# Residual on VectorE and the SyncE queue for one more kind of the last outputs of a fused attention and mixer block

## The chip, the cores and the metric

One Trainium2 chip, one core. TensorE multiplies matrices, VectorE and ScalarE work element by element, and SyncE and POOL (GpSimd) here mostly issue DMAs, which are copies between the memories; a DMA "lands" when its completion is signalled. The metric is the device time of one execution in microseconds (us), the median of several runs. A profile is one execution taken by the hardware profiler; its span (first to last instruction) is some 1.8 us shorter than the reported time.

## The reference, cut to what matters

```python
h  = x + A(layernorm(x))          # linear attention with an output projection, S=2048, D=1024
h2 = h + B(layernorm(h))          # token mixer: gelu(h^T @ w1 + b1) @ w2 + b2, F=3584
```

What matters is the last addition: every element of the output is the mixer's second product plus a bias b2, plus the residual `h`. The output is bf16, 2048 x 1024.

## The kernel before

`h` is written to the output tensor in DRAM half way through the kernel. The second product then works on "quads": two pairs of 128-row blocks, by a Strassen-like scheme with seven products. A pair `p` gives four outputs of 128 x 512, named by (`sh`, `dh`): row block and column half. Most of them are added to the residual by the DMA itself (an accumulating write, which the kernel issues from POOL). In the last quad, the two outputs of kind (1, 0), which come last of all, are treated otherwise: the residual is fetched back from DRAM ahead of time, VectorE adds it, and SyncE issues a plain write.

```python
def fetch(self, sh, dh):                       # read the residual into dead rows of an old weight tile
    t = odd[self.p - 2][:, 0:2, :].rearrange("p a b -> p (a b)")
    i = 2 * self.p + sh
    hd.dma_start(t, o_dram[i * P:(i + 1) * P, dh * CW:(dh + 1) * CW])      # SyncE
    self.hr[sh, dh] = t

def out(self, sh, dh, a, b, op):
    i = 2 * self.p + sh
    if (sh, dh) in self.hr:
        r = 2 + 2 * (a > 0)
        ot = odd[self.p - 2][:, r:r + 2, :].rearrange("p a b -> p (a b)")
    else:
        ot = ots.pop(0)
        ots.append(ot)
    op(ot[:, a:b], b2_sb[:, i:i + 1])          # evacuation with bias: ScalarE, or VectorE for kind (1, 1)
    to = o_dram[i * P:(i + 1) * P, dh * CW + a:dh * CW + b]
    if (sh, dh) in self.hr:
        dve.tensor_tensor(ot[:, a:b], ot[:, a:b], self.hr[sh, dh][:, a:b], ALU.add)
        nc.sync.dma_start(to, ot[:, a:b])
    else:
        nc.gpsimd.dma_start(to, ot[:, a:b], accum_op=ALU.add)              # POOL
# ... in run2, for the last quad only (cut is not None):
                sts[-1].split(cut)             # the very last output in 384 and 128 columns
                for st in sts:
                    st.fetch(1, 0)
```

`dve` and `hd` keep VectorE and SyncE instructions in program order. The kinds come in the order (1, 1), (0, 0), (0, 1), (1, 0); the (0, 1) evacuations of the two pairs stand on both sides of the last addition of a small product (`psI`) on VectorE.

## Time and profile before

| | kernel before |
|---|---|
| time, median of 3 runs | 560.86 us (560.84 to 561.08) |
| span of the profile | 559.3 us |
| TensorE busy | 553.0 us (99%) |
| end of the last matmul to end of span | 4.49 us |
| POOL DMA issues of outputs | 30 |

TensorE never waits between 40 us and its last matmul, so the time is the start-up, a solid block of matmuls, and a **tail**: from the end of the last matmul group in the timeline (551.65 + 3.20 = 554.85) to the end of the span (559.35). The lines themselves stand in the prediction. (The prediction counts 4.9 us, from 554.48. That is where the chain leaves TensorE for the 384-column part of the last output; the matmuls of the 128-column part run on to 554.86, and the 0.59 us of ScalarE read there belong to the 384 columns.)

### The profile page before, as it was taken

Reading aid. Unit: us, or ns where it says so; the run is one execution under the profiler, and the core shown is the slowest. Engines: PE = TensorE matmul, PEld = TensorE weight load, DVE = VectorE, ACT = ScalarE, POOL = GpSimd, SP = SyncE. Lnnn points to the kernel's source line nnn. Section 1 sums busy time; section 2 is a strip of 40 time slices with the busy share of each in tenths; the row PEclk is TensorE's granted clock in tenths of the full one; section 3 lists DMA queues with packets and bytes.
Section 4 is the critical chain, followed back from the end, with each engine's and each line's share of the span. In section 5 each row is a group of like instructions: output and inputs, shape, how many; then the busy total and the mean of one; then the engine's idle time right before and its main releaser. Section 6 shows DMA issues by size and latency. Waiting matters only on the chain.

```text
span 559.3 us, 8827 instructions
## 1 busy us (share of the span) xinstructions
PE 553.0 (99%) x3339; PEld 316.2 (57%) x3339; DVE 435.3 (78%) x848; ACT 291.1 (52%) x617; POOL 28.0 (5%) x38
## 2 busy tenths in 40 slices
PE   8999999999999999999999999999999999999996
PEld 3444444454444444456766766666444667667664
DVE  6898888544777688889989789887997879749745
ACT  5747677766767877646456465464210413413222
POOL 1000000000000000000000000000002103103112
PEclk9999999999999999999999999999999999999999
DMA  9933342115774762102240440413869649849334
GB/s 306 297 76 76 80 90 39 19 36 203 223 203 136 241 202 76 75 1 85 69 150 5 147 134 18 151 46 88 206 203 237 197 137 245 206 131 229 86 95 66
DMA packets 83627, 74.25 MB, mean 133 GB/s; under 512 B 15602, under 2 KB 76032, under 8 KB 83584
## 3 DMA queue, kind: packets, MB, share of 16 engines
q1 hardware_dynamic: 78528, 69.09, 41.1%
q0 software_dynamic: 4384, 3.95, 5.3%
q10 hardware_dynamic: 672, 0.66, 0.3%
q8 instruction: 26, 0.43, 0.3%
q14 instruction: 17, 0.14, 0.1%
HBM read 58.86 MB, written 11.67 MB: 126 GB/s over the span
## 4 chain that ended last, share of the span: by engine, by line
PE 97%; DVE 2%; ACT 1%; issue 0%; DVEq 0%
PE psI L230 25%; PE acc_t L230 18%; PE psC L230 16%; PE psB L230 8%; PE psB L945 4%; PE psC L945 4%; PE psA L945 4%; PE acc_t L869 2%; PE acc_t L1231 2%; PE psB L342 2%; PE psA L342 2%; PE psE L945 2%; PE psC L342 2%; PE psA L230 1%; PE kvps L898 1%; PE psE L342 1%
## 5 line engine op out<-in xcount | busy, mean ns | idle before, releaser
L230 PEld LDWEIGHTS <-is 128*128 128x128 f16 x736 | 71.8, 98 | 31.2 <-DVE hi L230 0.4
L230 PEld LDWEIGHTS <-sa 128*128 128x128 f16 x606 | 59.2, 98 | 27.1
L230 PEld LDWEIGHTS <-wq 128*128 128x128 bf16 (+1 forms) x496 | 48.5, 98 | 28.1 <-issue 1.0
L230 PE MATMUL acc_t<-wo_sb,pqT 128*128 128x512 f16 x256 | 55.6, 379 | 0.0
L488 POOL DMA_DIRECT2D out_dram<-wq x30 | 26.1, 927 | 525.4 <-ACT wq L491 495.0
L230 PE MATMUL acc_t<-xnT,wq_sb 128*128 128x512 bf16 x192 | 43.4, 379 | 0.0
L230 PEld LDWEIGHTS <-pqT 128*128 128x128 bf16 x256 | 25.0, 98 | 30.5 <-issue 0.6
L193 DVE TENSOR_SCALAR e_sb<-e_sb 128x512 bf16<-128x512 bf16 x64 | 18.6, 290 | 28.7 <-ACT e_sb L189 28.1
L230 DVE TENSOR_TENSOR t<-psI,t 128x256 f32<-128x256 f32 (+1 forms) x45 | 20.8, 475 | 22.2 <-PE psI L230 20.9
L189 ACT ACTIVATE e_sb<-acc_t 128x512 bf16<-128x512 f32 x40 | 23.9, 597 | 24.5 <-PE acc_t L230 12.0
L230 PE MATMUL psC<-gs,wq 128*128 128x512 f16 x140 | 34.1, 379 | 0.0
L945 PEld LDWEIGHTS <-xs 128*128 128x128 f16 x208 | 20.0, 98 | 23.4 <-DVE xs L931 1.3
L230 PEld LDWEIGHTS <-wq_sb 128*128 128x128 bf16 x192 | 18.5, 98 | 23.0 <-issue 1.3
L230 PE MATMUL psC<-hT,sa 128*128 128x512 f16 x112 | 31.2, 379 | 0.0
L230 PE MATMUL psI<-hi,is 128*128 128x256 f16 x200 | 30.0, 273 | 0.0
L230 PE MATMUL psB<-hT,sa 128*128 128x512 f16 x112 | 29.7, 379 | 0.0
L230 DVE BATCH_NORM_STATS2 hst<-acc_t 128x6 f32<-128x512 f32 x32 | 21.4, 692 | 9.0 <-ACT h_bf L230 8.9
L945 PE MATMUL psA<-wkv,xnT 128*128 128x512 bf16 x104 | 26.7, 379 | 0.0
L945 PEld LDWEIGHTS <-xnT 128*128 128x128 bf16 x156 | 15.2, 98 | 18.5 <-issue 0.2
L230 PE MATMUL psC<-hT,wq 128*128 128x512 f16 x96 | 24.6, 379 | 0.0
L230 ACT CAST h_bf<-acc_t 128x512 bf16<-128x512 f32 x32 | 18.4, 582 | 11.9 <-PE acc_t L230 11.5
L230 ACT COPY psI<-psI 128x256 f32<-128x256 f32 x50 | 18.0, 360 | 11.6 <-PE psI L230 9.7
(229 smaller groups left out, 1090.2 us busy)
## 6 DMA issues: line engine op xcount, KB each, us to landing
wq<-in_B_w_dram SPq DMA_DIRECT2D x14, 1024.0 KB, 8.0
wq<-in_B_w_dram SPq DMA_DIRECT2D x12, 896.0 KB, 7.1
gs<-parked SPq DMA_DIRECT2D x9, 896.0 KB, 4.6
xr<-in_A_x_dram SPq DMA_DIRECT2D x16, 256.0 KB, 5.9
rdb<-rd_dram SPq DMA_DIRECT2D x32, 128.0 KB, 3.8
out_dram<-h_bf SPq DMA_DIRECT2D x16, 256.0 KB, 2.0
x_sb<-in_A_x_dram SPq DMA_DIRECT2D x15, 256.0 KB, 3.0
out_dram<-wq POOLq DMA_DIRECT2D x30, 128.0 KB, 4.7
```

The costliest lines, as they stand in the source:

```text
L189: pin(nc.scalar.activation(e_sb[:], src, ACT.Exp))
L193: pin(nc.vector.tensor_scalar(e_sb[:], e_sb[:], 1.0, PHI_EPS, ALU.min, ALU.add))
L230: return (lambda *a, **kw: pin(op(*a, **kw))) if self.always or getattr(Held, self.key) else op
L342: pe.matmul(ps[:, cols], lhsT=lhs[:, k, :], rhs=mv(k)[:, cols], start=(start and k == 0), stop=(k == self.nk - 1), skip_group_check=True,)
L488: nc.gpsimd.dma_start(to, ot[:, a:b], accum_op=ALU.add)
L869: mm = nc.tensor.matmul(pp[:, 0:CW], lhsT=xnT[:, kt, i * P:(i + 1) * P], rhs=wkv[:, kt, c * CW:(c + 1) * CW], start=(kt == 0), stop=(kt == ...
L898: pin(nc.tensor.matmul(kv_ps[b][:, sl, :], lhsT=pks[i % NPK][:, j * P:(j + 1) * P], rhs=vaugs[i % NVA][:, j, :], start=False, stop=(i == N ...
L945: pin(nc.tensor.matmul(ps[:], lhsT=lhs[:, k, :], rhs=rhs[:, k, :], start=(start and k == 0), stop=(k == hk2 - 1), skip_group_check=True,))
L1231: nc.tensor.matmul(qp[:, 0:SW], lhsT=wq_sb[:, kt, j * P:(j + 1) * P], rhs=xnT[:, kt, u * SW:(u + 1) * SW], start=(kt == 0), stop=(kt == ND ...
```

## The change

Its intent: take the last accumulating writes out of the tail, by giving the kind (0, 1), last but one, the treatment that (1, 0) has. The whole diff:

```diff
-            t = odd[self.p - 2][:, 0:2, :].rearrange("p a b -> p (a b)")
+            t = odd[self.p - 2][:, 6 * dh:6 * dh + 2, :].rearrange("p a b -> p (a b)")
...
-                r = 2 + 2 * (a > 0)
+                r = 6 * dh + 2 + 2 * (a > 0)
...
                 for st in sts:
+                    st.fetch(0, 1)
                     st.fetch(1, 0)
```

Two accumulating POOL writes go; two SyncE reads, two VectorE additions and two SyncE writes come.

## The prediction

> **What bounds the kernel now.** I read the page first (busy shares, then the chain that ended last), then that chain again for the last 9 us alone, then the timeline of the same stretch engine by engine, then the DMA view for its last 3.3 us, and last the instructions of the program's closing line (L1739), which carries the end barrier.
>
> ```profile
> PE 553.0 (99%) x3339; PEld 316.2 (57%) x3339; DVE 435.3 (78%) x848; ACT 291.1 (52%) x617; POOL 28.0 (5%) x38
> ...
> PE 97%; DVE 2%; ACT 1%; issue 0%; DVEq 0%
> ```
>
> The first line is busy time per engine, the second the chain's shares. TensorE is busy for 553 of 559.3 us and makes up 97% of the chain; the clock row of the page is full in every slice. The change touches no matmul. So only two places can pay: a stall of TensorE, or the tail after its last matmul. The chain of the last 9 us, in order of time, shows where the tail begins:
>
> ```profile
> 551.82 2.66 PE psC L230 x14
> 554.48 0.02 issue
> 554.50 0.59 ACT wq L491
> 555.09 0.02 issue
> 555.12 0.36 DVE wq L230
> 555.48 0.14 DVEq L1739
> ```
>
> The matmuls end at 554.48; ScalarE adds the bias to the last output (0.59), VectorE adds the residual (0.36), and this view then stops, because transfers are not instructions. The span ends at 559.3, so 3.7 us of the tail are writes and barrier. The timeline (start, length, engine, line) gives the writes:
>
> ```profile
> 551.60 1.49 ACT L491 ACTIVATE wq<-e,b_sb 128x512 bf16<-128x512 f32 x2 [5.33 <-DVE e L230]
> 551.65 3.20 PE L230 MATMUL psC<-gs,w2o 128*128 128x512 f16 x21
> 551.85 0.42 DVE L230 TENSOR_TENSOR e<-psI,e 128x256 f32<-128x256 f32 x1 [0.29 <-PE psI L230]
> 552.61 1.75 POOL L488 DMA_DIRECT2D out_dram<-wq  x2 [5.29 <-ACT wq L491]
> 553.37 0.69 ACT L491 ACTIVATE wq<-psC,b_sb 128x512 bf16<-128x512 f32 x1 [0.28 <-PE psC L230]
> 554.09 0.43 DVE L230 TENSOR_TENSOR wq<-wq 128x512 bf16<-128x512 bf16 x1 [1.81 <-ACT wq L491]
> 554.50 0.84 ACT L491 ACTIVATE wq<-psC,b_sb 128x384 bf16<-128x384 f32 x2 [0.45 <-PE psC L230]
> 554.54 1.81 SPq L486 DMA_DIRECT2D out_dram<-wq  x3
> ```
>
> The two POOL issues at 552.61 are the accumulating writes that the change removes. In the trace they land at 555.70 and 557.21, and their packets are on the DMA engines until 556.84. The three SyncE writes (128, 96, 32 KB), issued at 554.54, 555.50 and 555.94, land at 557.39, 557.72 and 557.88. So the last landing is the 32 KB write's, but both kinds share the engines, as the DMA view of the last stretch shows (q0 is POOL's queue, q1 SyncE's):
>
> ```profile
> q1 hardware_dynamic: 420, 0.25, 25.2%
> q0 software_dynamic: 71, 0.06, 10.9%
> issues: line engine op xcount, KB each, median us to landing
> out_dram<-wq SPq DMA_DIRECT2D x1, 32.0 KB, 1.9
> ```
>
> After 557.88 comes the end barrier. In the instructions of L1739 (duration min/median/max in ns, first and last start in us):
>
> ```profile
> L1739 SPq EVENT_SEMAPHORE  x9: 17/28/28, 557.2 to 558.3; - x9
> ...
> L1739 POOLq DRAIN  x1: 5204/5204/5204, 553.4 to 553.4; - x1
> ```
>
> SyncE checks nine pairs of DMA semaphores one after another, some 0.06 us apiece, and is through at 558.40; POOL's drain, begun at 553.36, lasts 5.20 us and ends at 558.56, later than SyncE. The barrier steps after it take the span to 559.35.
>
> **What the Trainium skill says.** "DMA: Bandwidth & Descriptors", section Anatomy of one DMA, puts the fixed cost of a DMA at about 2 us, most of it the write receipt. The trace is a little below: 1.70 to 1.73 us for the 128 KB writes of the reciprocals to DRAM by SyncE, 2.0 us for the 256 KB residual writes in a quiet stretch. The same page, section Queues, rings and completion order, says that each DMA engine serves its queues in turn, packet by packet. The trace agrees in effect: the 128 KB write at 554.54 took 2.85 us beside POOL's packets. "Perfetto Trace Analysis", section DMA Instruction — SWDGE (GPSIMD), says that the profiled time of a POOL DMA is descriptor generation, not movement: here 0.86 us shown, 3.1 and 3.8 us to landing. "VectorE: DVE Perf Modes", section on the SBUF errata, measures a fixed term near 150 cycles; with two bf16 elements a cycle, 512 columns are an estimate of (150 + 256)/0.96 = 423 ns, and the trace has 0.43 us.
>
> **The change part by part.** The instruction order of the changed build, compared with the old one, is the same on TensorE; only the end of the others differs.
>
> *Fetches.* Two more 128 KB reads of the residual beside two of the same size, issued by SyncE near 537.8 at 0.47 us each. They queue behind the 896 KB reload of gs (issued 537.38, landed 542.18; first wanted by TensorE at 544.03), so they delay it little, and they are wanted only at 552.3. By the landings of the present two (542.52, 542.85) the new ones land near 543.5. Cost on the path: 0. The new tiles lie in weight rows that are already dead.
>
> *VectorE.* Two additions of 0.43 us, in program order. The first comes before the last psI sum, which now waits for ScalarE: add 552.35 to 552.78 (ScalarE ends the first output at 552.32), sum to about 553.12 (was 552.28), second activation 553.15 to 553.88 (was 552.36 to 553.08). The psC activation waits for ScalarE, 553.8 to 554.5 instead of 553.37 to 554.05: 0.45 us later. The 384-column one still starts at 554.50, as its matmuls end at 554.48. The sum's bank is wanted by no later matmul. So the delay is used up just ahead of the last output: 0 to 0.1 us on the path.
>
> *SyncE issues.* Five writes instead of three: about 552.8, 554.4, 555.0, 555.50, 555.94. An issue takes 0.34 to 0.41 us, so the last two stay where they are.
>
> *POOL.* Two issues of 0.87 us go, and its drain starts some 6 us earlier.
>
> *Landing of the last write.* Without POOL's packets, a quiet SyncE write shows its first packet 0.83 us after issue and lands 0.35 us after its last packet (a residual write at 217.64: packets 218.47 to 219.30, landed 219.65). The 32 KB write has 8 packets on each engine at 18 ns, 0.15 us; with some spread, 0.83 + 0.25 + 0.38 = 1.46 us instead of 1.94: landing at 557.40 instead of 557.88, **-0.48**.
>
> *End barrier.* SyncE's DMAs take the eight hardware semaphores in turn. The last write has the second of them now; four more issues move it to the sixth. In the present trace six more checks follow its own; then there will be two: 4 x 0.06 = **-0.25**. And POOL's drain, if it depends only on POOL's own DMAs, no longer ends after SyncE: 558.56 against an arrival of about 558.43, **-0.13**.
>
> Sum: -0.48 - 0.25 - 0.13 + 0.05 = -0.81 us at the most optimistic. I don't give the drain and the landing their full value and take -0.65: 560.86 - 0.65 = 560.2.
>
> **The rivals.** (1) The landing is hidden anyway: the 32 KB write is a receipt-bound write that POOL's traffic hardly touches (1.94 us against 1.70 for a bigger one in quiet). Then only the barrier pays, 0.1 to 0.4 us: 560.5 to 560.8. (2) The serial chain between VectorE and ScalarE becomes the end: if the activations follow each other with more delay than I counted, the last two SyncE issues slip by 0.1 to 0.4 us and eat the gain: 560.5 to 561.0. For it: four handovers between the two engines now stand in a row before 554.5. Against it: about 0.45 us of idle ScalarE time before 554.50 covers them. (3) The extra reads delay the gs reload and TensorE stalls near 544: up to 0.6 us for 256 KB at the 430 GB/s seen then, so about 561.4; against it, 1.85 us of slack and the order of issue.
>
> **Range and chances.** The whole tail after the last matmul is 4.9 us of 560.86; 2% is 11.2 us. No part of the change can give that, and none adds it. Runs of the kernel before differ by 0.24 us, so I take 559.8 to 560.7: the low end is the full sum and a bit of luck between runs, the high end rival 1 or 2 with little left. Faster by over 2%: 0.01; within 2%: 0.985; slower: 0.005.
>
> **What would show it.** Right: matmuls still end near 554.5; POOL's last issue is near 546; five SyncE writes, the last issued within 0.1 us of 555.94, with a landing near 1.5 us; span near 558.6. Wrong: a TensorE gap between 542 and 546 (rival 3), a last SyncE issue after 556.1 (rival 2), a 32 KB landing still at 1.8 us or more (rival 1), or a POOL drain that ends just after SyncE's checks again, which would mean that it never was a cost of its own.

## The result, and the profile after

| | before | after |
|---|---|---|
| median of 3 runs | 560.86 us (560.84 to 561.08) | 560.33 us (560.04 to 561.04) |
| ratio, 95% interval | | 0.9992 (0.9969 to 1.0014) |
| the same, timed again (9 and 6 runs) | 561.02 us (560.31 to 561.79) | 560.22 us (560.01 to 562.66) |
| ratio, 95% interval | | 0.9984 (0.9970 to 0.9997) |
| span of the first profile | 559.3 us | 558.3 us |
| tail of the first profile | 4.49 us | 3.65 us |

A ratio is the mean time of one kernel's runs over that of the other's of the same rounds, so not quite the ratio of the medians. As point estimates the gain is 0.5 to 0.9 us, within 2%. The first interval includes no gain at all; the second goes from 0.2 to 1.7 us.

The timeline of the kernel after, in the stretch and with the columns of that shown before (start, length, engine, line, operation, count, idle time before it):

```profile
551.36 0.72 ACT L491 ACTIVATE wq<-e,b_sb 128x512 bf16<-128x512 f32 x1 [5.33 <-DVE e L230]
551.42 3.20 PE L230 MATMUL psC<-gs,w2o 128*128 128x512 f16 x21
552.12 0.42 DVE L230 TENSOR_TENSOR wq<-wq 128x512 bf16<-128x512 bf16 x1 [0.79 <-ACT wq L491]
552.46 0.42 DVE L230 TENSOR_TENSOR e<-psI,e 128x256 f32<-128x256 f32 x1
552.57 3.52 SPq L486 DMA_DIRECT2D out_dram<-wq  x5
552.91 0.72 ACT L491 ACTIVATE wq<-e,b_sb 128x512 bf16<-128x512 f32 x1 [0.83 <-DVE e L230]
553.54 1.57 ACT L491 ACTIVATE wq<-psC,b_sb 128x512 bf16<-128x512 f32 x3
553.67 1.00 DVE L230 TENSOR_TENSOR wq<-wq 128x512 bf16<-128x512 bf16 x2 [0.79 <-ACT wq L491]
554.88 0.49 DVE L230 TENSOR_TENSOR wq<-wq 128x384 bf16<-128x384 bf16 x2 [0.22 <-ACT wq L491]
```

There is no POOL line any more, and five SyncE writes instead of three. VectorE, ScalarE and VectorE wait for one another in turn (0.79, 0.83, 0.79 us), as the order of instructions had it. Yet the 384-column activation starts 0.35 us ahead of the last matmul's end in both kernels, and the last VectorE pair 0.26 us after it in both: the handovers were absorbed.

The DMA view from 555.8 us to the end, and the instructions of the program's closing line (duration min/median/max in ns, then first and last start in us):

```profile
q1 hardware_dynamic: 353, 0.18, 25.3%
issues: line engine op xcount, KB each, median us to landing
out_dram<-wq SPq DMA_DIRECT2D x1, 32.0 KB, 1.6
```

```profile
L1740 SPq EVENT_SEMAPHORE  x10: 17/28/28, 556.1 to 557.6; - x10
L1740 POOLq DRAIN  x3: 51/102/5622, 545.8 to 558.0; - x3
```

POOL's queue q0 is gone from the last stretch; the 32 KB write lands 1.6 us after its issue instead of 1.9. POOL's long drain begins at 545.8 and is over 5.6 us later, long before the end.

All 14 profiles can be put into one table. Times are in us from the end of the last matmul: issue of the last write, how long it takes to land, when SyncE is through its checks of the DMA semaphores (the counters that a landing raises; two short drains of SyncE are counted in), when POOL's drain ends (one instruction of the program's closing line, on which POOL stays until after its own last DMA has landed), and the tail. Where POOL's drain was over before the last matmul, there is a dash.

| kernel | issue | landing takes | SyncE through | drain ends | tail |
|---|---|---|---|---|---|
| before | 1.08 | 1.94 | 3.55 | 3.70 | 4.49 |
| before, again | 1.08 | 1.70 | 3.31 | 3.52 | 4.31 |
| after | 1.03 | 1.57 | 2.88 | - | 3.65 |
| after, again | 1.03 | 1.56 | 2.87 | - | 3.64 |
| before, checks turned by four | 1.04 | 1.75 | 3.07 | 3.32 | 4.11 |
| after, plain writes by POOL | 1.08 | 1.73 | 3.22 | 3.29 | 4.08 |
| after, one tiny late POOL write | 1.03 | 1.57 | 2.88 | 2.96 | 3.75 |
| second pair only | 1.07 | 1.57 | 3.04 | 2.20 | 3.81 |
| after, turned by two | 1.03 | 1.57 | 2.76 | - | 3.53 |
| after, turned by three | 1.03 | 1.57 | 3.18 | - | 3.95 |
| after, one more VectorE addition | 1.41 | 1.57 | 3.26 | - | 4.04 |
| after, last write from ScalarE | 0.79 | 1.75 | 2.82 | - | 3.59 |
| after, one operation per output | 0.73 | 1.56 | 2.55 | - | 3.32 |
| all three together | 0.61 | 1.63 | 2.40 | - | 3.17 |

One rule, read off these profiles, fits every row to 0.01 us: the tail is 0.745 us (the barrier, from POOL's step that waits for everybody to the end of the span) after the later of two arrivals, SyncE through its checks plus 0.025, or POOL's drain plus 0.045. In the kernel before, and in the three experiments whose last POOL DMA is issued within 1.5 us of the last matmul's end, it is POOL's; else SyncE's.

### The profile page after: what moved, and what is told of

Same layout as the page of the kernel before. It is cut to its first block, busy times and chain, and to the rows that moved or that the text cites. A ratio compares the mean times of both kernels' runs of the same rounds, so it can differ in the third digit from the quotient of the medians.

```text
span 558.3 us, 8814 instructions
## 1 busy us (share of the span) xinstructions
PE 551.9 (99%) x3323; PEld 315.8 (57%) x3339; DVE 436.1 (78%) x850; ACT 291.0 (52%) x617; POOL 26.3 (5%) x36
## 4 chain that ended last, share of the span: by engine, by line
PE 95%; DMA 2%; DVE 2%; issue 1%; ACT 0%; DVEq 0%
PE psI L230 25%; PE acc_t L230 18%; PE psC L230 16%; PE psB L230 8%; PE psC L946 4%; PE psB L946 4%; PE psA L946 4%; PE psB L342 2%; PE psA L342 2%; PE acc_t L1232 2%; PE psE L946 2%; DMA x_sb<-in_A_x_dram 2%; PE psC L342 2%; PE acc_t L870 2%; PE psA L230 1%; PE kvps L899 1%
## 5 line engine op out<-in xcount | busy, mean ns | idle before, releaser
L488 POOL DMA_DIRECT2D out_dram<-wq x28 | 24.4, 928 | 519.8 <-ACT wq L491 489.5
```

## The experiments

My theory: the tail has two paths in parallel. POOL: last POOL write, landing, drain. SyncE: last write, landing, checks. The change takes POOL out, and makes SyncE's path shorter by quiet engines and by fewer checks after the last landing. Rivals: the 0.5 us are noise of the start; it is the accumulating kind of DMA that costs, whatever the queue; the drain only follows SyncE.

### Both kernels again

No edit. The kernel after was timed in five rounds; the kernel before was profiled once more.

> The changed kernel again, timed in five rounds. The tail is counted from the end of the last matmul group in the timeline to the end of the span: 4.50 us in the kernel before (554.85 to 559.35), 3.65 in the one profile of the changed kernel (554.62 to 558.27). My theory (the 0.85 us are a fixed saving in the tail): tail 3.6 to 3.7 again, ratio of times 0.9980 to 0.9990, whole interval below 1. Rival (the 0.5 us between the medians are run to run noise of the front, as runs of 560.04, 561.04 and 560.33 suggest): tail between 3.7 and 4.5, ratio 0.9995 to 1.0005.

> The kernel before once more, for a second tail. If tails are fixed by the program: 4.45 to 4.55 us, last write issued 1.1 us after the last matmul's end, landing 1.9 us later, POOL's drain ending after SyncE's checks. If they vary from run to run as the whole times do: off by 0.2 us or more.

The tail of the kernel after came out as 3.64, 0.01 from the first, and the ratio as 0.9984 with an interval below 1: theory. The tail of the kernel before was 4.31, not 4.45 to 4.55. That is the first miss, and a useful one: issue and checks were the same to 0.01 us, but POOL's last write landed 2.17 us after the last matmul instead of 2.36, and SyncE's last one took 1.70 instead of 1.94. So in these two pairs the landings vary in the kernel with POOL's writes (1.94, 1.70) and hardly in the one without (1.57, 1.56).

In the longest run, which happened to be profiled, the start is to blame. The run of the kernel after that was profiled here took 562.66 us; its waits of TensorE name the place:

```profile
PE acc_t L870 <- DMA wkv<-in_A_wqkv_dram: 2.2, 1, 2.2
PE acc_t L98 <- DVE warm L88: 1.2, 1, 1.2
PE psB L946 <- DVE xs L932: 0.3, 1, 0.3
```

The first line, 2.2 us of waiting for the first weights, is absent in all other profiles but one, the plain writes by POOL below, where it is 0.3 us. Comparing the start of the same ScalarE instruction in this profile and the first one of the kernel after, the shift is 2.6 us at 30 us and still 2.6 us at the end. Between the first profiles of before and after it is 0.23 us, at 30 us and at the end alike. So of the 1.08 us between those two spans, 0.23 come from the start, which the change doesn't touch, and 0.85 are the change.

### Turning the order of the checks in the kernel before

SyncE's DMAs take eight hardware semaphores in turn, and at the end the semaphores are checked in a fixed order. Four dead reads (8 KB each; nobody uses what they bring) shift which one the last write has.

```diff
                 for st in sts:
                     st.fetch(1, 0)
+                for k in range(4):
+                    hd.dma_start(odd[sts[0].p - 2][:, 12, 32 * k:32 * (k + 1)], x[0:P, 32 * k:32 * (k + 1)])
```

> The kernel before with four tiny dead reads by SyncE ahead of its last writes, so that the last write has the sixth semaphore in turn as in the changed kernel, and two checks follow its own instead of six. SyncE should be through its checks about 0.28 us after the last landing, not 0.53. Theory (POOL's drain depends only on POOL's own DMAs, some 1.3 us after the last of them lands, and gates the end): tail unchanged, 4.45 to 4.55. Rival (the drain only follows SyncE, so the checks set the end): tail 4.2 to 4.3.

SyncE was through 0.28 us after its last landing instead of 0.53, at 3.07. The end did not follow it: POOL's drain ended 0.25 us later, at 3.32, and the tail was that plus 0.79. From the closing line:

```profile
L1741 SPq DRAIN  x3: 7/7/13, 557.9 to 558.5; - x3
L1741 POOLq DRAIN  x2: 102/2460/4819, 553.4 to 558.4; - x2
L1741 POOLq EVENT_SEMAPHORE  x2: 17/17/17, 558.2 to 558.3; - x2
```

SyncE's first drains stand at 557.9; POOL's long one runs from 553.37 for 4.82 us to 558.19, and the barrier step that waits for everybody (POOL EVENT_SEMAPHORE) comes right after it, at 558.2. So the drain doesn't follow SyncE, and by the order of arrivals a shorter row of checks alone gains nothing in the kernel before, as long as POOL's drain is later. The tail itself doesn't show that: it was 4.11, below the 4.45 to 4.55 of the theory and even below the 4.2 to 4.3 of the rival, since POOL's last write landed at 1.97 this time. Whether the dead reads had a part in this, one profile can't say. In all three profiles of this family the drain ends 1.35 us after that landing.

### Plain writes by POOL

```diff
-                nc.sync.dma_start(to, ot[:, a:b])
+                (nc.gpsimd if dh else nc.sync).dma_start(to, ot[:, a:b])
```

> The changed kernel, whose two (0,1) outputs take the residual on VectorE as there, but leave by POOL as plain writes (result right). Theory (the gain comes from POOL being out of the tail: its packets beside the last write and its late drain): POOL's last issue is near 1 us before the last matmul's end, lands some 2 to 3 us later, drain 1.3 us after that; landing of the last write 1.6 to 1.9 us; tail 4.2 to 4.7. Rival (the gain comes from the accumulating kind of DMA being gone, whatever the queue): tail 3.6 to 3.9.

The tail was 4.08, between the two ranges: 0.12 below the theory's, 0.18 above the rival's. POOL's two issues, from the timeline (the last matmul ends at 555.26 here):

```profile
553.48 0.57 POOL L486 DMA_DIRECT2D out_dram<-wq  x1 [5.74 <-DVE wq L230]
555.03 0.56 POOL L486 DMA_DIRECT2D out_dram<-wq  x1 [0.98 <-DVE wq L230]
```

The second one is issued 1.24 us later against the last matmul than in the kernel before, as it waits for VectorE's addition, but it lands after 2.18 us instead of 3.83, so POOL is done 0.2 to 0.4 us earlier (landing at 1.94 against 2.36 and 2.17). The accumulating kind does cost landing time here, but without it half of the gain or more is still missing: the tail is 0.43 us longer than that of the kernel after. Not all of this is the drain. This version has SyncE's last write on the fourth semaphore (four checks after its own), which accounts for 0.12; its landing is 0.17 longer and its issue 0.05 later; by the rule above only the last 0.10 are the drain's, which arrives that much after SyncE.

### One tiny late POOL write

```diff
                 nc.sync.dma_start(to, ot[:, a:b])
+                if dh and self.p % 2:
+                    nc.gpsimd.dma_start(dram.tile([P, 32], BF16, name="scratch")[:], ot[:, 0:32])
```

> The changed kernel with one tiny (8 KB) POOL write to a scratch tensor after the second (0,1) output's addition, so POOL's drain is late again, with hardly any packets beside the last write. Theory (drain about 1.3 us after the last POOL landing): issue some 0.5 us before the last matmul's end, landing about 2 us later, so the drain ends some 3.3 to 3.8 us after the last matmul, beyond SyncE's 2.9, and the tail is 4.1 to 4.7. Rival (the drain is no gate of its own): tail 3.65.

```profile
554.66 0.56 POOL L488 DMA_DIRECT2D scratch<-wq  x1 [7.29 <-DVE wq L230]
```

The write was issued 0.23 us ahead of the last matmul's end, landed 1.89 us later, and the drain ended 1.31 us after that, at 2.96, just past SyncE's 2.88. The tail was 3.75: longer than 3.65 by the 0.10 that the drain's arrival is later, and the write of 8 KB left the last landing at 1.57. Direction and mechanism are the theory's; the size is not, and the expectation's own sum was wrong: issue at -0.5, landing 2 us later and 1.3 us of drain give 2.8, not 3.3 to 3.8. By its terms the drain would have ended just ahead of SyncE; it came just behind, as the write was issued 0.27 us later than I put it.

### Half of the change

```diff
                 for st in sts:
-                    st.fetch(0, 1)
+                    if st is sts[1]:
+                        st.fetch(0, 1)
                     st.fetch(1, 0)
```

> Half of the change: only the second (0,1) output takes the residual on VectorE and leaves by SyncE; the first stays with the accumulating POOL DMA, issued about 2.2 us before the last matmul's end and landed 3.1 us later as before, so the drain ends near 2.2 us after the last matmul, ahead of SyncE's checks. The last write has the fourth semaphore: four checks after its own. Theory: landing of the last write 1.6 to 1.8 us, tail 3.65 + 0.12 + 0 to 0.2 = 3.8 to 4.0. Rival (one accumulating write in the tail costs half as much as two, by the packets alone): tail 4.05 to 4.1.

Tail 3.81, at the low end. One accumulating write remains, but it is issued 2.24 us ahead of the last matmul's end; its drain is over at 2.20 and the last landing takes 1.57, as if POOL weren't there. The difference of 0.16 to the kernel after is mainly two more checks (0.12). So only the later one of the two POOL writes was in the tail; the gain isn't shared out in halves.

### Turning the order of the checks in the kernel after

The same dead reads as above, two and three of them, behind the fetches of the kernel after.

> The changed kernel with two tiny dead reads more by SyncE ahead of the last writes: the last write moves from the sixth to the eighth semaphore, none of the pairs is checked after its own. Theory (checks in a fixed order, 0.06 us each, after the last landing): tail 3.65 - 0.12 = 3.53, SyncE through its checks 0.16 us after the landing. Rival (the order of the checks is hidden by something else, so that the shorter row of checks in the changed kernel was no gain): tail 3.65.

> Three dead reads more instead of two: the last write wraps to the first semaphore, so that seven checks follow its own. One read more than the run before would cost 0.43 us. Theory: tail 3.65 + 5 x 0.06 = 3.96. Rival (checks are hidden): 3.65. That a mere 4 KB read near 540 us does it by traffic is excluded by the run before, which has two of them.

3.53 and 3.95, against 3.53 and 3.96 expected (a read is 8 KB, not the 4 KB that the expectation says). Two reads shorten the tail by 0.12 us, a third one lengthens it by 0.43. Without POOL's drain the checks are on the path, 0.06 us apiece.

### One more addition on VectorE

```diff
                 dve.tensor_tensor(ot[:, a:b], ot[:, a:b], self.hr[sh, dh][:, a:b], ALU.add)
+                if dh and self.p % 2 == 0:
+                    dve.tensor_tensor(odd[self.p - 2][:, 12:14, :].rearrange("p a b -> p (a b)"), ot, self.hr[sh, dh], ALU.add)
```

> The changed kernel with one more VectorE addition of 0.43 us (into a dead tile) right after the first (0,1) output's, to measure how far the row of handovers between VectorE and ScalarE was from the path. In the changed kernel ScalarE stands idle 0.06 us ahead of the 384-column activation, and can overlap its start by 0.1 us more. If the delay of 0.45 us that the change brings is absorbed with only that to spare (my reading): the last write is issued about 0.25 us later, 1.25 to 1.35 us after the last matmul's end, tail 3.85 to 3.95. If there is more slack: tail 3.65. If VectorE's delay goes through in full: 4.05 or more.

The last issue moved by 0.38 us to 1.41 and the tail to 4.04: worse than I read it, nearly all of the 0.43 us went through. The change used up the slack of that row of handovers to within some 0.05 us.

### Versions that go further

Last write from ScalarE's queue (`(nc.scalar if a else nc.sync).dma_start(to, ot[:, a:b])`):

> The changed kernel with the very last write (128 columns, 32 KB) issued from ScalarE's queue, which is idle by then, instead of behind the 96 KB write on SyncE, where it waits about 0.25 us for the issue before it. Theory (the path is now VectorE, issue, landing, checks): issue 0.79 us after the last matmul's end instead of 1.03, landing 1.55 us, tail 3.40. Rival (the DMA engines or the descriptor hardware take the writes one after another, so an earlier issue lands no earlier): tail 3.65.

The issue came at 0.79, as expected, but the landing took 1.75 instead of 1.57, and of 0.25 us only 0.06 were left: 3.59, nearer to the rival's 3.65 than to the 3.40 of the theory. The Trainium skill, "DMA: Bandwidth & Descriptors", section Rules for kernel authors, says that spreading DMAs over queues only saves issue time, since all run on the same 16 engines; this run fits that, as 0.24 us of issue time were saved and the landing came only 0.06 us earlier. I first took the 96 KB write, issued 0.14 us before, to be in its way, but that isn't shown: in the trace's packets the last write's are spread over 0.30 us against 0.27 in the kernel after, and most of the delay comes after its last packet (0.47 us to landing against 0.35). The other version with ScalarE's queue, the last one below, has 0.48 there, all profiles without POOL and with SyncE alone 0.35. Why is open.

One VectorE operation per output, which adds bias and residual in one go and takes ScalarE out:

```diff
+            if (sh, dh) in self.hr:
+                ... # ot, i as in out()
+                dve.scalar_tensor_tensor(ot[:, a:b], ps[:, a:b], b2_sb[:, i:i + 1], self.hr[sh, dh][:, a:b], ALU.add, ALU.add)
+                nc.sync.dma_start(o_dram[i * P:(i + 1) * P, dh * CW + a:dh * CW + b], ot[:, a:b])
+                return
```

> The changed kernel with bias and residual of the four outputs in one VectorE operation each instead of a ScalarE and a VectorE operation. Theory (after the change the end hangs on ScalarE, VectorE, issue, landing in a row; a one-step evacuation shortens it): 384 columns done 0.25 us after the last matmul's end, 128 columns at 0.5, last issue 0.65, landing 1.56, tail 3.25; ratio to the kernel before 0.9970 to 0.9985. Rival (VectorE, now with 3 us of such work before the end, becomes late): last issue after 1.0, tail 3.65 or more.

```profile
553.69 0.75 DVE L230 SCALAR_TENSOR_TENSOR wq<-psC,b_sb,wq 128x512 bf16<-128x512 f32 x1
554.87 0.88 DVE L230 SCALAR_TENSOR_TENSOR wq<-psC,b_sb,wq 128x384 bf16<-128x384 f32 x2 [0.43 <-issue]
```

Tail 3.32 (0.07 over the expectation, the last issue came at 0.73 instead of 0.65). One operation of 0.75 us does what 0.69 and 0.43 us on two engines did. Time 560.17 us, ratio to the kernel before 0.9983 (0.9971 to 0.9994).

All together, with two dead reads for the order of the checks:

> All together: one VectorE operation per output, the last write from ScalarE's queue, two tiny dead reads that move the last write to the last semaphore that is checked. Theory (the three gains add): last issue 0.53, landing 1.56, through the checks 0.16 later, tail 3.0 to 3.1, that is 1.2 to 1.5 less than the kernel before and 0.6 less than the changed one; ratio to the kernel before 0.9965 to 0.9980. Rival (they overlap): tail as in the better of the two runs before, 3.25.

Tail 3.17, a little over the expectation, and 559.73 us, ratio 0.9978 (0.9965 to 0.9991): the fastest version here, by 0.48 us of tail against the kernel after. In times the two were not run in the same rounds, and their intervals against the kernel before overlap. In this one's profile TensorE waited 0.6 us between 470 and 530 us, in a stretch that the edit doesn't touch; one profile can't say whether that is chance.

## Why the prediction was right or wrong

The number was right, in part by luck, as the terms below show: 560.2 predicted in a range of 559.8 to 560.7, 560.33 and 560.22 measured. The range on single runs is another matter: two runs of the kernel after took 561.04 and 562.66. The second lost its time in the start-up, which I had not looked into; the first wasn't profiled.

- **Nothing moves in the matmuls.** Right. TensorE waits for nothing between 40 us and its last matmul in either kernel.
- **Fetches cost nothing.** Right. The reload of gs landed 4.69 us after its issue against 4.80, and the four reads, of which the first and the third are new, between 542.20 and 543.27, by the 543.5 estimated.
- **Handovers are absorbed, 0 to 0.1 us.** Right, the last issue came even 0.05 us earlier against the last matmul. But the margin that I called covered was all used up: one more addition went through nearly in full.
- **Landing, -0.48.** Right in kind, off in size: 1.57 us instead of 1.46. What it is compared with isn't fixed: 1.94 in the first profile, 1.70 in the second. So the term is -0.37 or -0.14. Its working took 0.83 us to the first packet, 0.25 of spread and 0.38 after the last packet, where its own example has 0.35; the trace of the kernel after has 0.94, 0.27 and 0.35. And the last write's packets did not share the engines with POOL's: in both profiles of the kernel before POOL's were through at 1.98 and 1.81 us after the last matmul, ahead of its first one at 2.03. What lay beside it in place of them is SyncE's own 96 KB write, whose packets ended at 2.52 and 2.21 there and at 1.93 in the kernel after.
- **Checks, -0.25.** Right: 0.53 to 0.28 us, and the turned versions gave 0.06 us for each position.
- **Drain, -0.13.** 0.17 in the first profile and 0.23 in the second. It begins 7.3 us earlier against the last matmul, not 6. Here is the step that read the profile in a skewed way. I took SyncE's path, whose write lands last, as the path, and the drain as a small extra at its end. The runs show the opposite for the kernel before: the drain ends it in both profiles, 1.35 us after POOL's last landing, and SyncE's landing and checks lie beside it. With the checks alone shortened, the drain was still what ended last. The sum still came out, because in the kernel after SyncE's path is the one that counts, and the sum of my terms is the distance from the old end to the end of that path.
- **The discount.** I cut -0.81 to -0.65 for doubt about landing and drain. The two pairs of profiles give -0.85 (4.49 to 3.65) and -0.67 (4.31 to 3.64), the two timings -0.53 and -0.80 by medians. That the full sum of -0.81 comes so near to the first pair is luck: the landing was put 0.11 too high, and the issue, 0.05 earlier where 0.05 of delay was charged, made up for it.
- **The rivals.** The hidden landing and the stall by the reads didn't come. Rival 1 called the last write bound by its receipt; of its 1.57 us 0.94 pass before its first packet and 0.35 after its last. The chain of VectorE and ScalarE didn't become late, but was next to it.

What stays open: why the landings spread (1.70, 1.73, 1.75, 1.94). With a 128 KB POOL write in flight until 1.9 us or later they are 1.70 or more, in the SyncE-only profiles 1.56 or 1.57. In the first profile of the kernel before nearly all of the extra 0.37 us is in the spread of the last write's packets (0.61 against 0.27), beside the late 96 KB write; in the second 0.10 of 0.13 comes after its last packet. That POOL's packets made the 96 KB write late is likely, as it was late in all four such profiles (its packets ended at 2.12 to 2.52 against at most 1.95 in the others that issue it at the same moment), but no run shows it alone.

## What to carry to other kernels

Where the last matmul is followed by some us of writes, draw the end as paths in parallel, each queue with its landing and what the barrier waits for after it, and see which arrives last; here a POOL DMA near the end held a drain open for 1.3 us past its landing. As long as that arrives last, shortening the other path gains nothing; in this kernel, once it was gone, every tenth on the other path counted: fewer engines in a row for the last evacuation, and which semaphore the last write has. Compare such changes by the tail of the profile, not by the whole time, where the start-up can vary by more than the gain (2.6 us here).

## What the Trainium skill lacked or had wrong

- Drain of POOL at the end of a program (no page tells it; "Perfetto Trace Analysis" names DRAIN only as an instruction of the sequencer alone): it ended 1.27 to 1.35 us after the last landing of a POOL DMA in all 14 profiles, also behind an 8 KB write.
- Cost of an accumulating write ("DMA: Bandwidth & Descriptors" says who may issue it and what may not run beside it, but gives no time): in the tail, 128 KB from POOL landed in 3.1 to 3.8 us accumulating, in 2.0 and 2.2 us plain, though issued at other moments.
- Time from issue to landing of a SyncE write: the same page gives a formula, with a fixed cost of about 2 us, for POOL's kind of DMA alone (section Anatomy of one DMA — SWDGE (gpsimd) path). Plain SyncE writes to DRAM in a quiet tail took 1.57 us for 32 KB and 1.7 to 1.8 us for 128 KB in all.
- Checks of the DMA semaphores at the program's end: no page has them. Here they run one after another on SyncE, 0.06 us each, so that the semaphore of the last write is worth up to 0.43 us.
